# Attention and feed-forward on one core: local units by pairs, turned with 32-row transfers and VectorE from the fourth batch on

## The chip, the cores and the metric

The kernel runs on one core of one Trainium2 chip. The time is device time in microseconds (us), from the start of the program to its end. The core has five engines that run side by side, each with its own queue in program order: TensorE (PE in the profile; PEld are its weight loads), VectorE (DVE), ScalarE (ACT), GpSimd (POOL) and SyncE (SP), which issues all transfers here. TensorE writes into PSUM only.

## The reference, cut to what matters

There are 8 batches of 8 heads, 576 positions and 64 numbers a head. Each batch gets two attentions, whose outputs are added: one over means of 4 neighbouring positions, repeated 4 times, and a local one, in which a position sees those less than 4 away. The sum goes through a feed-forward layer with a gate of its own.

```python
q_d, k_d, v_d = means over 4 positions
out_up = np.repeat(sm_attn(q_d, k_d, v_d), 4, axis=2)
mask = np.abs(pos[:, None] - pos[None, :]) < 4
scores = np.where(mask, scale * (q @ k.T), -1e9)
out_local = softmax(scores) @ v
x = (out_up + out_local)                 # 4608 tokens, 512 wide
h = x @ w_in                             # 1024 wide
solu = h * softmax(h)
ln = (solu - mean) / np.sqrt(var + 1e-6) * g_ln
return ln @ w_out
```

## The kernel before

**Feed-forward.** The 4608 tokens are 36 tiles of 128. `ffn_in(i)` makes h_i with 24 matmuls of 128x512 (L770): x and w_in are each split into a high part and a rest, and three of the four products are kept (xh·wi_h, xh·wi_l, xl·wi_h). VectorE takes the maximum of a row (nmx, L778), ScalarE the exponential (e, L782), VectorE the product with h (L785); then the PSUM tile h, of which there is one, is free for the next tile. The mean is taken off (L807), and the tile goes to memory and back in another order (u, L813, and v, L845), where VectorE turns it in blocks of 32x32 (L866). `ffn_ut` splits it (uh on ScalarE, L872; the rest ul, L874, on GpSimd, on VectorE from tile 29 on), and `ffn_out(i)` makes o_i with 24 matmuls (L888). ScalarE scales the result (osb, L895).

**Local attention.** A window is 64 positions; a unit is two windows, and a batch has five units. `Local.by_tensor` works on one unit, all 8 heads: 16 matmuls of 64x64 for the scores (sc, L614), the mask added by VectorE (L632), the maximum (L637), its subtraction on GpSimd (L639), the exponential (L641), the sum and its reciprocal (L644, L648), the product on GpSimd (L650). Then TensorE turns the probabilities with four transposes of 128x128 (plt, L660), ScalarE copies them out of PSUM (plT, L663), 16 matmuls of 64 rows by 58 or 56 columns multiply them with v (xp, L670), and the result goes into x (L496 or L498). `Local.by_blocks` stands in the source, but `ON_TENSOR = 8` sends every batch to `by_tensor`.

**Pooled attention** goes by pairs of heads (`Pooled`: sd L696, mxd L703, pd L711 and L720, pdt L731, pdT L738 to L743, po L752). The sums of four v are made by GpSimd (`pooled_vsum`, L434 and L437). Batches 0 and 1 get q and k turned by TensorE (qp, kp, L478), the others by VectorE (L411, L415).

**Weights.** `Weights.piece` turns 16 pieces of the float64 weights into a high part and a rest, with four steps on VectorE (L325 to L338), a product with g_ln for w_out (L358), a rounding (L360) and a difference on GpSimd (L362).

**Order.** The program is a list of small steps (`plan`), and the table `ORDER` says by number in which order they are issued. Every engine runs its own instructions in that order and waits where an input isn't there. Two matmuls of zeros at 24 places (`keep_clock`, L947) keep TensorE at work early on.

Of the kernel before, what the change touches and what calls it, by code (L numbers as in the profile page):

```python
# [129 lines left out]
def pooled_local_attention_then_solu_ffn(  # L130
# [34 lines left out]
    QN = SD // QC  # L165


    TILES = ((0, 0), (1, 1), (0, 1), (1, 0))

    EARLY = 2  # L170
    MASKED = 0
    W_PSUM = False
    WARM = 24

    def rows(n):
        return slice(n * 64, n * 64 + 64)

# [864 lines left out]
```

## Time and profile before

| | |
|---|---|
| median of 3 runs | 602.74 us (602.57 to 603.37) |
| profiled execution | 602.74 us, of which the span from the first to the last instruction is 601.0 us |
| ACT busy | 361.8 us, 60% of the span |
| POOL busy | 375.6 us, 62% |
| transfers | 203,913 packets, 94.34 MB, 157 GB/s on average |
| granted TensorE clock | 0.989 on average |

Busy time is time in which an engine has an instruction at work. Busy alone does not say that an engine sets the time: that is read from whether it waits, and from who waits for it.

### The profile page before, as it was taken

Reading aid. Unit: us, or ns where it says so; the run is one execution under the profiler, and the core shown is the slowest. Engines: PE = TensorE matmul, PEld = TensorE weight load, DVE = VectorE, ACT = ScalarE, POOL = GpSimd, SP = SyncE. Lnnn points to the kernel's source line nnn. Section 1 sums busy time; section 2 is a strip of 40 time slices with the busy share of each in tenths; the row PEclk is TensorE's granted clock in tenths of the full one; section 3 lists DMA queues with packets and bytes.
Section 4 is the critical chain, followed back from the end, with each engine's and each line's share of the span. In section 5 each row is a group of like instructions: output and inputs, shape, how many; then the busy total and the mean of one; then the engine's idle time right before and its main releaser. Section 6 shows DMA issues by size and latency. Waiting matters only on the chain.

```text
span 601.0 us, 15341 instructions
## 1 busy us (share of the span) xinstructions
PE 574.8 (96%) x5912; PEld 447.1 (74%) x5912; DVE 396.5 (66%) x692; ACT 361.8 (60%) x800; POOL 375.6 (62%) x553
## 2 busy tenths in 40 slices
PE   6889789899999999999999999999999999999996
PEld 3666557677777777787877777777777878788785
DVE  5989999869747677766856767737655533643541
ACT  3758866577745566566664854657465655553443
POOL 2576668867784778678574777656786767332221
PEclk8979999899999999999999999999999999999999
DMA  8999776687769767766878567847416623124230
GB/s 231 238 251 254 140 183 146 164 178 162 195 144 189 171 167 186 170 148 175 190 151 201 143 173 182 185 114 195 97 59 188 146 89 114 63 88 151 96 123 35
DMA packets 203913, 94.34 MB, mean 157 GB/s; under 512 B 162496, under 2 KB 192704, under 8 KB 203840
## 3 DMA queue, kind: packets, MB, share of 16 engines
q1 hardware_dynamic: 203840, 93.37, 63.3%
q8 instruction: 46, 0.75, 0.6%
q14 instruction: 27, 0.22, 0.1%
HBM read 65.54 MB, written 27.79 MB: 155 GB/s over the span
## 4 chain that ended last, share of the span: by engine, by line
PE 75%; POOL 6%; DVE 5%; ACT 4%; SPq 4%; DMA 3%; issue 3%; POOLq 0%; DVEq 0%
PE o L888 31%; PE h L770 27%; PE xp L670 3%; PE plt L660 3%; PE po L752 3%; PE sc L614 2%; DMA qm<-in_q_dram 2%; SPq L245 2%; PE pdt L731 2%; PE sd L696 2%; POOL pl L639 2%; DMA v<-u 1%; SPq L264 1%; POOL pd L720 1%; DVE w L334 1%
## 5 line engine op out<-in xcount | busy, mean ns | idle before, releaser
L888 PE MATMUL o<-wo_h,uh 128*128 128x512 f32 x288 | 117.9, 409 | 0.8 <-ACT uh L872 0.7
L770 PE MATMUL h<-wi_h,xh 128*128 128x512 f32 x288 | 116.3, 404 | 0.6 <-DVE e L785 0.6
L770 PE MATMUL h<-wi_h,xl 128*128 128x512 f32 x288 | 114.3, 397 | 1.3 <-POOL xl L922 1.3
L888 PE MATMUL o<-wo_l,uh 128*128 128x512 f32 x288 | 114.5, 398 | 0.0
L770 PE MATMUL h<-wi_l,xh 128*128 128x512 f32 x288 | 114.1, 396 | 0.0
L874 POOL TENSOR_TENSOR ul<-v,uh 128x512 fp32r<-128x512 f32 x58 | 74.4, 1288 | 19.7 <-ACT uh L872 7.7
L778 DVE TENSOR_REDUCE nmx<-h 128x1 f32<-128x1024 f32 x36 | 43.9, 1219 | 63.8 <-PE h L770 63.8
L888 PE MATMUL o<-wo_h,ul 128*128 128x512 f32 x288 | 79.1, 396 | 0.4 <-DVE ul L874 0.4
L782 ACT ACTIVATE e<-h,nmx 128x1024 f32<-128x1024 f32 x36 | 40.0, 1112 | 51.0 <-DVE nmx L778 51.0
L888 PEld LDWEIGHTS o<-wo_h,uh 128*128 128x128 f32 x288 | 54.6, 190 | 15.6 <-ACT uh L872 1.4
L770 PEld LDWEIGHTS h<-wi_h,xl 128*128 128x128 f32 x288 | 54.2, 188 | 15.2 <-POOL xl L922 2.1
L770 PEld LDWEIGHTS h<-wi_h,xh 128*128 128x128 f32 x288 | 54.2, 188 | 14.8 <-issue 1.0
L888 PEld LDWEIGHTS o<-wo_h,ul 128*128 128x128 f32 x288 | 54.2, 188 | 14.0 <-DVE ul L874 0.8
L770 PEld LDWEIGHTS h<-wi_l,xh 128*128 128x128 f32 x288 | 54.3, 189 | 12.2
L888 PEld LDWEIGHTS o<-wo_l,uh 128*128 128x128 f32 x288 | 54.5, 189 | 11.8
L922 POOL TENSOR_TENSOR xl<-x,xh 128x512 fp32r<-128x512 f32 (+1 forms) x40 | 47.1, 1183 | 18.6 <-ACT xh L919 17.4
L807 ACT ACTIVATE e<-e,nmu 128x1024 f32<-128x1024 f32 x35 | 40.1, 1146 | 28.2 <-POOL nmu L790 28.1
L785 DVE SCALAR_TENSOR_TENSOR e<-h,e 128x1024 f32<-128x1024 f32 x36 | 43.7, 1214 | 19.9 <-ACT e L782 19.9
L650 POOL TENSOR_TENSOR pl<-pl,rsl 128x512 f32<-128x512 f32 x40 | 42.1, 1055 | 20.7 <-DVE rsl L648 18.2
L866 DVE STREAM_TRANSPOSE v<-v 128x512 f32<-128x512 f32 x70 | 46.3, 688 | 12.5 <-DMA v<-u 12.5
L872 ACT ACTIVATE uh<-v 128x512 fp32r<-128x512 f32 x70 | 42.9, 623 | 14.9 <-DVE v L866 11.0
L639 POOL TENSOR_TENSOR pl<-pl,mxl 128x512 f32<-128x512 f32 x40 | 41.8, 1052 | 9.0 <-DVE mxl L637 4.6
(95 smaller groups left out, 1076.1 us busy)
## 6 DMA issues: line engine op xcount, KB each, us to landing
u<-e SPq DMA_DIRECT2D x35, 512.0 KB
v<-u SPq DMA_DIRECT2D x140, 128.0 KB
vw<-in_v_dram SPq DMA_DIRECT2D x160, 64.0 KB
vs<-in_v_dram SPq DMA_DIRECT2D x32, 288.0 KB
out_dram<-osb SPq DMA_DIRECT2D x36, 256.0 KB
qm<-in_q_dram SPq DMA_DIRECT2D x96, 72.0 KB
km<-in_k_dram SPq DMA_DIRECT2D x96, 72.0 KB
w<-in_moe_w_out_dram SPq DMA_DIRECT2D x8, 512.0 KB
```

What stands on the lines that cost most here:

```text
L639: nc.gpsimd.tensor_tensor(out=pl, in0=pl, in1=max_bc, op=ALU.subtract)
L650: nc.gpsimd.tensor_tensor(out=pl, in0=pl, in1=rs.unsqueeze(3).broadcast_to([P, NPR, 2, W]), op=ALU.mult)
L770: nc.tensor.matmul(hps[:, n, :], src[:, cc, :], wt[:, cc, n * 512:(n + 1) * 512], start=(cc == 0 and src is xh and wt is wi_h), stop=(cc = ...
L778: nc.vector.tensor_reduce(out=nmx, in_=hf, op=ALU.max, axis=AX.X, negate=True)
L782: nc.scalar.activation(e, hf, AF.Exp, bias=nmx, scale=1.0, accum_out=se)
L785: nc.vector.scalar_tensor_tensor(out=e, in0=hf, scalar=1.0, in1=e, op0=ALU.mult, op1=ALU.mult, accum_out=su)
L807: nc.scalar.activation(e, e, AF.Identity, bias=nmu, scale=1.0)
L866: nc.vector.transpose(vg, vg)
L872: nc.scalar.activation(uh, tp, AF.Copy)
L874: (nc.vector if v is None or i in LATE else nc.gpsimd).tensor_tensor(out=ul, in0=tp, in1=uh.bitcast(F32), op=ALU.subtract)
L888: nc.tensor.matmul(o, src[:, j, :], wt[:, 4 * g + j, :], start=(g == 0 and j == 0 and src is uh and wt is wo_h), stop=(g == 1 and j == 3 a ...
L922: nc.gpsimd.tensor_tensor(out=l, in0=src, in1=h.bitcast(F32), op=ALU.subtract)
```

## The change

- For batches 3 to 7 units 0 and 1, and 2 and 3, go through a new class, `PairOfLocals`, two units at a time; unit 4 stays with `Local`. The scores of both units go into one tile `pl` of 128x1024, ordered by halves of 32 keys. Eight transfers of 32 rows by 512 numbers (64 KB each) bring each 32-row block to its place in `plT`, and one VectorE instruction of 128x1024 turns it in blocks of 32x32. The TensorE transposes of those units and the copies out of PSUM are gone; the product with v is 64 columns wide instead of 58. `by_blocks` is removed.
- `MASKED = 2`: in batches 0 and 1 TensorE adds the mask to the scores with two matmuls of 128x256; VectorE takes the maximum from PSUM and subtracts it, and GpSimd's subtraction falls away.
- `G_LATE`: for w_out the product with g_ln and the rounding are one ScalarE instruction, and the rest is one VectorE instruction.
- `OTHER` lists 133 steps in which an instruction goes to the other engine of two. With it GpSimd gives VectorE 27 of 58 `ul`, 19 of 40 `xl`, 11 of 32 `pd`, 10 of 32 pooled sums, and 14 subtractions and products of the local attention; ScalarE gives VectorE 14 of 39 first copies into x, 7 of 35 `e` less the mean, 2 `plT` and 2 `kT`, and takes 6 `pdT`; VectorE gives GpSimd 10 of the first steps (L325) of the 16 pieces of weights.
- `ORDER` is a new table from its first number to its last. The matmuls that keep TensorE at work now use the identity, and each place has a PSUM tile of its own name.

```diff
 ORDER = """
-181 0 182 1 2 3 165 25 183 166 4 5 6 184 167 185 24 26 186 187 188 27 7 8 173 32 168 169 170
+8 0 23 168 169 22 170 171 172 173 174 25 24 10 175 160 161 162 163 164 176 177 16 26 27 32 28
...
+OTHER = """
+37 53 59 93 178 186 202 210 242 250 258 266 274 282 471 482 524 541 543 549 566 568 574 643 671
...
-    MASKED = 0
+    MASKED = 2
...
+    def engine(usual, instead):
+        return instead if now[0] in other else usual
...
-                nc.scalar.activation(t, t, AF.Copy, scale=self.g[:, fc:fc + 1])
+                if G_LATE:
+                    nc.scalar.activation(hi, t, AF.Copy, scale=g)
+                    yield
+                    nc.vector.scalar_tensor_tensor(
+                        out=lo, in0=t, scalar=g, in1=hi.bitcast(F32), op0=ALU.mult, op1=ALU.subtract
+                    )
...
-    ON_TENSOR = 8
+    PAIRED = 3
...
+    class PairOfLocals:
...
+            pl = big(f"pl_{b}_{u}")
+            by_unit = pl.rearrange("p (c n h k) -> p c n h k", c=2, n=2, k=32)
+            for n in range(2):
...
+                        nc.tensor.matmul(
+                            at[rows(wi), par, pr],
+                            bt.qT[rows(par), pr, s0:s0 + W], bt.kT[rows(par), pr, s0:s0 + W],
+                            start=True, stop=True,
+                        )
...
+            plT = big(f"plT_{b}_{u}")
+            half = N * 32
+            for wi in range(2):
+                for a in range(2):
+                    for c in range(2):
+                        nc.sync.dma_start(
+                            plT[wi * 64 + c * 32:][0:32, a * half:(a + 1) * half],
+                            pl[wi * 64 + a * 32:][0:32, c * half:(c + 1) * half],
+                        )
+                yield
+            nc.vector.transpose(plT, plT)
+            yield
...
+                        nc.tensor.matmul(
+                            xp[rows(par), wi, pr * W:(pr + 1) * W],
+                            bt.vw[u + n][rows(wi), 2 * pr + par, :],
+                            plT[rows(wi), n, par * NPR + pr], start=True, stop=True,
+                        )
...
-            (nc.vector if v is None or i in LATE else nc.gpsimd).tensor_tensor(
+            usual = nc.vector if v is None or i in LATE else nc.gpsimd
+            (usual if v is None else engine(usual, nc.vector)).tensor_tensor(
                 out=ul, in0=tp, in1=uh.bitcast(F32), op=ALU.subtract
```

Three places show how the order moves. The last number of a name is that of its buffer; the two before it are the batch and the unit (or head pair), or the tile and its half.

**TensorE, between the output matmuls of tile 12 and the next input matmuls.** Before, the end of batch 4's local attention and the start of batch 5's:

```order
L670 MATMUL xp_4_2_4383<-plT_4_2_4259,vw_4_2_4041 64x58 x16
L660 MATMUL plt_4_3_4403<-ident_82,pl_3_108 128x128 x4
L670 MATMUL xp_4_1_4410<-plT_4_1_4127,vw_4_1_3485 64x58 x16
L614 MATMUL sc_5_1_4429<-kT_5_4137,qT_5_4321 64x64 x16
L660 MATMUL plt_4_4_4464<-ident_82,pl_0_105 128x128 x4
L670 MATMUL xp_4_3_4475<-plT_4_3_4408,vw_4_3_3570 64x58 x16
L614 MATMUL sc_5_0_4499<-kT_5_4137,qT_5_4321 64x64 x16
```

Now, at the same place, in the middle of tile 12's output:

```order
L753 MATMUL xp_4_2_4274<-plT_4_2_4120,vw_4_2_3310 64x64 x16
L607 MATMUL sc_5_4_4306<-kT_5_3930,qT_5_4117 64x64 x16
L655 MATMUL plt_4_4_4325<-ident_82,pl_0_107 128x128 x4
L823 MATMUL pdt_4_0_4331<-ident_82,pd_4_0_4100 72x64 x12
L695 MATMUL sc_5_0_4354<-kT_5_3930,qT_5_4117 64x2x32 x16
```

Of the transposes `plt` only that of unit 4 is left; the product `xp` of unit 2 is 64 columns wide.

**VectorE, from the maximum of tile 18 to the product that frees h.** Before:

```order
L778 TENSOR_REDUCE nmx_18_5044<-h_18_4939 128x1
L411 STREAM_TRANSPOSE kT_6_5055<-km_6_4452 128x576
L367 TENSOR_REDUCE kd_6_5057<-kT_6_5055 128x144
L411 STREAM_TRANSPOSE kT_6_5055<-km_6_4452 128x576 x2
L785 SCALAR_TENSOR_TENSOR e_18_5066,su_18_5069<-h_18_4939,e_18_5066 128x1024
```

Now, with the three instructions ahead of the maximum:

```order
L746 STREAM_TRANSPOSE plT_5_0_4865<-plT_5_0_4865 128x1024
L972 TENSOR_TENSOR ul_15_0_4877<-v_15_4781,uh_15_0_4876 128x512
L719 TENSOR_TENSOR pl_5_2_4757<-pl_5_2_4757,mxl_5_2_4818 128x1024
L870 TENSOR_REDUCE nmx_18_4927<-h_18_4893 128x1
L963 STREAM_TRANSPOSE v_16_4879<-v_16_4879 128x4x128
L913 RECIPROCAL r_16_4942<-se_16_4544 128x1
L639 TENSOR_REDUCE sml_5_4_4961<-pl_1_108 128x8
L643 RECIPROCAL rsl_5_4_4963<-sml_5_4_4961 128x8
L1020 TENSOR_TENSOR xl_19_4940<-x_4_4231,xh_19_4939 128x512
L972 TENSOR_TENSOR ul_15_1_4889<-v_15_4781,uh_15_1_4888 128x512
L913 RECIPROCAL r_17_4982<-se_17_4812 128x1
L877 SCALAR_TENSOR_TENSOR e_18_4994,su_18_4997<-h_18_4893,e_18_4994 128x1024
```

Three instructions that stood on GpSimd (`ul` twice and `xl`) are now in VectorE's row, two of them between maximum and product; ahead of the maximum stand a turn of `plT`, which waits for transfers, and a subtraction of 128x1024.

**SyncE at the same place**, where the transfers of `plT` stand. Now:

```order
L942 DMA v_15_4781<-u_15_4536 32x4x256 x4
L299 DMA vw_7_2_4846<-in_v_dram 64x8x64 x2
L741 DMA plT_5_0_4865<-pl_5_0_4353 32x512 x8
L942 DMA v_16_4879<-u_16_4775 32x4x256 x4
L286 DMA qm_6_4495<-in_q_dram 32x18x32 x4
L286 DMA km_6_4496<-in_k_dram 32x18x32 x4
```

Before, the transfers of v_16 followed loads of v and the output of tile 12:

```order
L264 DMA vw_6_4_4848<-in_v_dram 64x4x64 x4
L897 DMA out_0_dram<-osb_12_4518 128x512
L264 DMA vw_5_3_4864<-in_v_dram 64x4x64 x4
L845 DMA v_16_4933<-u_16_4844 32x4x256 x4
L264 DMA vw_5_1_4957<-in_v_dram 64x4x64 x4
```

The eight transfers stand ahead of those of v_16 and wait for the product of the pair on its engine; a load of `vw` now takes two transfers instead of four.

More of the change, by code (lines that the diff above doesn't have):

```diff
@@ L208, in pooled_local_attention_then_solu_ffn, with make_bands @@
         nc.vector.tensor_copy(out=mask_b, in_=mask)
-    if WARM:
-        zeros = cpool.tile([P, P], BF16, name="zeros")
-        nc.gpsimd.memset(zeros, 0.0)
+    if MASKED:
+        filler = ident_b
+    elif WARM:
+        filler = cpool.tile([P, P], BF16, name="filler")
+        nc.gpsimd.memset(filler, 0.0)
     mhalf = cpool.tile([P, 1], F32, name="mhalf")
     nc.vector.memset(mhalf, -0.5)
+    GR = SD // 2
+    BAND = {0: (0, 16), 1: (3, 15), 3: (1, 15)}
+    bands = {}
+    def make_bands():
+        t = moe.tile([P, DFF], F32, tag="e", name="bands")[:, 0:3 * 160]
+        t = t.rearrange("p (r x) -> p r x", r=3)
+        nc.gpsimd.memset(t, 0.0)
+        by_half = ident.rearrange("p (h k) -> p h k", h=2)
+        for n, (r, (off, m)) in enumerate(BAND.items()):
+            nc.vector.tensor_reduce(
+                out=t[:, n, GR:GR + m],
+                in_=by_half[:, :, off:off + FAC * m].rearrange("p h (j i) -> p j h i", i=FAC),
+                op=ALU.add, axis=AX.XY,
+            )
+            bands[r] = t[:, n]
     LP = 2 * W + 2
@@ L223, in pooled_local_attention_then_solu_ffn, with copy @@
     nc.vector.memset(qd_flat[:, NPR * SD:], 0.0)
+    other = {int(n) for n in OTHER.split()}
+    now = [None]
+    def engine(usual, instead):
+        return instead if now[0] in other else usual
+    def copy(eng, out, in_):
+        if eng is nc.scalar:
+            nc.scalar.activation(out, in_, AF.Copy)
+        else:
+            eng.tensor_copy(out=out, in_=in_)
     def two_banks(pool, tag, name):
@@ L433, in pooled_vsum, with pool_steps @@
             vs = self.vs.pop((c, hs.start))
[L434 removed]
+            eng = engine(nc.gpsimd, nc.vector)
+            eng.tensor_tensor(
                 out=vs[:, :, 0:2 * D], in0=vs[:, :, 0:2 * D], in1=vs[:, :, 2 * D:4 * D], op=ALU.add
             )
[L437 removed]
+            eng.tensor_tensor(
                 out=self.vd[:, c, hs], in0=vs[:, :, 0:D], in1=vs[:, :, D:2 * D], op=ALU.add
             )
+        def pool_steps(self):
+            firsts = [-(-s0 // FAC) for s0 in starts]
+            ends = firsts[1:] + [SD]
+            for c in range(2):
+                tp = two_banks(ps_h, "h", f"vp_{self.b}_{c}")[0:GR]
+                at = tp.rearrange("p h (r a d) -> p h r a d", r=NPR, a=2)
+                ws = range(5 * c, 5 * c + 5)
+                for w in ws:
+                    s0, g0, g1 = starts[w], firsts[w], ends[w]
+                    at0 = GR - (g0 - GR * c)
+                    K = FAC * g1 - s0
+                    for half in range(2):
+                        nc.tensor.matmul(
+                            at[:, half, :, half ^ (w % 2), :],
+                            bands[s0 % FAC][half * W:half * W + K, at0:at0 + GR],
+                            self.vw[w // 2][half * W:half * W + K, w % 2],
+                            start=w == ws[0], stop=w == ws[-1],
+                        )
+                yield
+                vd = self.vd[:, c].rearrange("p h d -> p (h d)")
+                nc.scalar.activation(vd, tp[:, 0], AF.Copy)
+                yield
+                nc.vector.tensor_tensor(out=vd, in0=vd, in1=tp[:, 1], op=ALU.add)
+                yield
     class EarlyBatch(Batch):
@@ L806, in ffn_in @@
         else:
-            nc.scalar.activation(e, e, AF.Identity, bias=nmu, scale=1.0)
+            if engine(nc.scalar, nc.vector) is nc.scalar:
+                nc.scalar.activation(e, e, AF.Identity, bias=nmu, scale=1.0)
+            else:
+                nc.vector.tensor_scalar(
+                    out=e, in0=e, scalar1=1.0, scalar2=nmu, op0=ALU.mult, op1=ALU.add
+                )
         s = small.tile([P, 1], F32, tag="s", name=f"s_{i}", bufs=6)
@@ L940, in pooled_local_attention_then_solu_ffn @@
     weights = Weights()
-    idle = []
     def keep_clock(n):
-        if not idle:
-            idle.append(ps_o.tile([P, 512], F32, tag="o", name="warm"))
+        o = ps_o.tile([P, 512], F32, tag="o", name=f"warm_{n}")
         for _ in range(2):
             nc.tensor.matmul(
-                idle[0].rearrange("p (a n) -> p a n", n=P), zeros,
-                zeros.unsqueeze(1).broadcast_to([P, 4, P]), start=True, stop=True,
+                o.rearrange("p (a n) -> p a n", n=P), filler,
+                filler.unsqueeze(1).broadcast_to([P, 4, P]), start=True, stop=True,
             )
@@ L981, in attention @@
     def attention(bt):
-        values(bt)
-        local = [Local(bt, u, bt.b > 0) for u in range(5)]
-        pooled = [Pooled(bt, pr, bt.b == 0) for pr in range(NPR)]
-        for it in pooled + local if bt.b == 0 else local + pooled:
-            if isinstance(it, Local):
+        by_pe = bt.b < SUMS_ON_PE
+        late = bt.b == 0
+        if bt.b < PAIRED:
+            local = [Local(bt, u, not late) for u in range(5)]
+        else:
+            local = [PairOfLocals(bt, 0, not late), PairOfLocals(bt, 2, not late), Local(bt, 4, not late)]
+        pooled = [Pooled(bt, pr, late) for pr in range(NPR)]
+        if by_pe:
+            if not bt.b:
+                step(make_bands)
+            for u in range(5):
+                step(bt.load_v, u)
+            row(bt.pool_steps(), 6)
+        else:
+            values(bt)
+        for it in pooled + local if late else local + pooled:
+            if isinstance(it, PairOfLocals):
+                step(bt.load_v, it.u)
+                step(bt.load_v, it.u + 1)
+                row(it.steps(), 16)
+                continue
+            if isinstance(it, Local) and not by_pe:
                 step(bt.load_v, it.u)
```

206 lines of the change are left out of this document (103 added, 103 removed), and 199 rows, old and new, of tables (ORDER, OTHER).

## The prediction

> **What bounds the kernel now.** I read the page's busy shares first, then the busy times of chosen stretches, then the chain of work that ended last. In the stretches each engine has its busy time and, in brackets, its instructions; after them stand TensorE's granted clock and the share of the transfer engines.
>
> ```profile
> span 601.0 us, 15341 instructions
> PE 574.8 (96%) x5912; PEld 447.1 (74%) x5912; DVE 396.5 (66%) x692; ACT 361.8 (60%) x800; POOL 375.6 (62%) x553
> ...
> 0.00:120.00 120.00, 100.16 (x1546) 74.08 (x1547) 106.38 (x182) 79.46 (x182) 77.54 (x89) 0.94 0.85 201
> 120.00:555.00 435.00, 433.63 (x4192) 340.84 (x4191) 272.28 (x484) 262.88 (x587) 290.07 (x439) 1.00 0.62 152
> ...
> 20.00:60.00 40.00, 34.78 (x687) 26.79 (x684) 36.10 (x67) 30.15 (x89) 25.75 (x25) 0.91 1.02 247
> 60.00:110.00 50.00, 41.18 (x558) 31.21 (x550) 48.94 (x82) 36.65 (x75) 35.91 (x38) 1.00 0.73 162
> ...
> 142.40:354.30 211.90, 211.56 (x2156) 166.46 (x2154) 142.57 (x253) 131.88 (x299) 148.89 (x218) 1.00 0.73 172
> ```
>
> From 120 to 555 us TensorE is idle for 435 - 433.6 = 1.4 us: it is the bound there, and what leaves its queue leaves the time. A busy share alone wouldn't say so, since matmuls overlap, but the chain agrees, with TensorE at 75% of the span. The first 120 us are another stage: TensorE is idle for 20 us, transfers are at their limit up to 60 us (share 1.02), and VectorE is at 98% from 60 to 110 us (48.94 of 50).
>
> ```profile
> PE 75%; POOL 6%; DVE 5%; ACT 4%; SPq 4%; DMA 3%; issue 3%; POOLq 0%; DVEq 0%
> ```
>
> I sum against the execution's own time of 602.74 us: a span of 601.0 and 1.7 around it. It is also the median of the three runs.
>
> **Transposes that go.** Start times of TensorE groups (start, length, line):
>
> ```profile
> 360.45 0.66 PE L660 MATMUL plt<-ident,pl 128*128 128x128 f32 x4
> 361.04 1.16 PE L614 MATMUL sc<-kT,qT 64*64 64x64 f32 x64
> 362.13 0.66 PE L660 MATMUL plt<-ident,pl 128*128 128x128 f32 x4
> 362.71 0.69 PE L670 MATMUL xp<-plT,vw 64*64 64x56 f32 x32
> 363.33 0.50 PE L888 MATMUL o<-wo_h,uh 128*128 128x512 f32 x1
> ...
> 350.81 0.66 PE L660 MATMUL plt<-ident,pl 128*128 128x128 f32 x4
> 351.22 0.47 PE L888 MATMUL o<-wo_h,uh 128*128 128x512 f32 x1
> ```
>
> From start to next start, the four transposes of a unit take 0.41 to 0.59 us. Five batches lose them for four units each: 20 x 0.5 = **-10.0 us** (-8.2 to -11.8). All of them fall after 120 us, in the stage that TensorE bounds. The product xp takes 0.62 us at 56 columns (362.71 to 363.33); the scores, with 64, take 1.09 / 2 = 0.55. Width hardly shows; going by 64/58 of 0.5, I add 20 x 0.04 = **+0.8** (0 to 1.4). That the new scores are written in runs of 32 I cost at nothing, as no row shows such a write.
>
> **Early masks.** Each of ten units gets two matmuls of 128x256 in bf16. The nearest row:
>
> ```profile
> 20.73 1.90 PE L947 MATMUL warm<-zeros 128*128 128x512 bf16 x8
> 22.56 1.21 PE L478 MATMUL qp<-ident,qm 96*64 96x96 f32 x24
> ```
>
> (22.56 - 20.73) / 8 = 0.23 us for 512 columns, so 0.115 for 256, and 20 of them take 2.3 us. They lie where TensorE has 20 us to spare; about half will hide: **+1.2** (0 to 2.3).
>
> **The start.** What leaves the path there is GpSimd's subtraction in batches 0 and 1. Pieces of the chain:
>
> ```profile
> 2.10 8.49 DMA qm<-in_q_dram
> ...
> 31.93 1.00 POOL pl L639
> ...
> 33.80 0.97 POOL pl L639
> ...
> 35.90 2.00 POOL pl L639 x2
> ...
> 111.24 3.81 PE o L888 x12
> ```
>
> Four of them, 4.0 us, stand in the chain. The first q also gets one 512 KB piece of weights less ahead of it on SP; it now lands 8.5 us after the start, with 1.6 MB up to and including it, so a third less is worth up to 2.7 us. Against it, VectorE, 98% busy, receives eight rests of w_out (8 x 0.77 = 6.1 us) and gives ten first steps (10 x 0.81 = 8.1 us), but gets copies and differences too: counted up to the second half of o_0 its order holds some 4 us more than before. Between -6 (both gains in full) and +4 (VectorE's extra in full) I take **-2.5**, nearer the gains because four of these links are in the chain by name.
>
> **VectorE.** This is the unknown term. Its rows:
>
> ```profile
> L866 DVE STREAM_TRANSPOSE v<-v 128x512 f32<-128x512 f32 x70 | 46.3, 688 | 12.5 <-DMA v<-u 12.5
> L632 DVE TENSOR_TENSOR pl<-sc,mask 128x512 f32<-128x512 f32 x40 | 26.7, 675 | 12.8 <-PE sc L614 12.7
> L498 DVE TENSOR_TENSOR x<-x,xp 128x464 f32<-128x464 f32 x4 | 2.5, 624 | 0.4 <-PE xp L670 0.4
> L325 DVE TENSOR_SCALAR w<-w 128x512 f32<-128x512 f32 x16 | 12.9, 814 | 5.6 <-ACT w L323 5.6
> L874 DVE TENSOR_TENSOR ul<-v,uh 128x512 fp32r<-128x512 f32 x12 | 9.0, 765 | 7.6 <-ACT uh L872 5.5 <-issue 2.1
> ```
>
> Over the whole program it gains: 10 turns of 128x1024 at 2 x 0.688 (13.8 us); 27 ul and 19 xl, six of them halves, 43 x 0.765 (32.9); 14 subtractions and products, seven of double width, 21 x 0.675 (14.2); 11 pd of 432 columns (6.3); ten pairs of pooled sums, 1.5 x 0.675 each (10.1); 14 copies into x and 4 others (11.4); 7 e of double width (9.5); w_out 6.1. It loses 8.1 of L325 and six copies pdT (2.7). Sum: +93 us on 396.5. Neighbours overlap a little (two turns in a row take 1.31 us, not 1.38), so some +88.
>
> ```profile
> 133.34 1.31 DVE v L866 x2
> ```
>
> It is not spread evenly. From the start of h_5 (142.4 us) to that of h_20 (354.3) VectorE was busy for 142.6 of 211.9 us. In the new order the same stretch of tiles holds 15 ul, 4 xl, 5 wide turns, 14 halves of subtraction or product, 6 pd, 5 pooled sums, 6 copies, 2 e and some ten turns and sums of q, k and v that come earlier: by the rows above 54, with the overlap 51 us. TensorE's stretch loses ten transposes and shrinks to about 207 us. So VectorE stands at 194 of 207, 94%, where it was at 67%. GpSimd falls from 149 to about 101 and ScalarE loses 22 copies; they can't be the bound.
>
> What that costs depends on how full VectorE can run. The stretch from 60 to 110 us shows 98%: 194 / 0.98 = 198, under 207, and costs nothing. That from 20 to 60 us shows 36.10 of 40, 90%: 194 / 0.9 = 215, and costs 8. I take the middle, **+4** (0 to 22, see the third rival).
>
> Where it would bite: h has one PSUM tile, so h_19 waits for VectorE's product on h_18.
>
> ```profile
> L778 DVE TENSOR_REDUCE nmx<-h 128x1 f32<-128x1024 f32 x36 | 43.9, 1219 | 63.8 <-PE h L770 63.8
> L785 DVE SCALAR_TENSOR_TENSOR e<-h,e 128x1024 f32<-128x1024 f32 x36 | 43.7, 1214 | 19.9 <-ACT e L782 19.9
> ...
> 222.88 5.62 PE o L888 x24
> ```
>
> Between h_18 and h_19 TensorE has only o_15, 5.62 us. VectorE's maximum and product take 2.4; between them the order has a turn (0.69), a sum (0.68), xl and ul (1.53) and three reciprocals (0.5): 5.8 us, some 5.5 with the overlap. So there the slack is gone, where the old order had sd, pdt and plt as well. Tiles 9, 13, 20 and 23 have as little. The turn of plT also waits on VectorE for its transfers, with ul_15 and the maximum behind it. The nearest transfers, the four of v with the same 512 KB, took 5.45 us in the chain; waits for v cost VectorE 12.5 us in all (the row of L866).
>
> ```profile
> 318.20 5.45 DMA v<-u
> ```
>
> On SP the eight transfers wait for the pair's product, with v_16, q and k queued behind; before tile 20 such a delay meets tiles of slack, so I put it inside the +4.
>
> **Sum.** 601.0 - 10.0 + 0.8 + 1.2 - 2.5 + 4 = 594.5; with the 1.7 around it **596 us**.
>
> **Rivals.** *First, nothing waits.* The transposes are worth their upper end (-11.8), VectorE keeps up (0) and the start gains 4: 601 - 11.8 + 0.8 + 1.2 - 4 = 587.2, so 589 us (584 to 591). For it: TensorE ran 435 us with 1.4 idle while VectorE waited for h alone for 63.8 us, so there is slack to spend. Against it: the 94%.
>
> *Second, the saving comes back as waiting.* TensorE loses its 10 us of work and waits 8 to 13 us longer; time 600.5 to 604.5. This is also the case where transposes are swapped for waits on transfers and the change does not do what it says.
>
> *Third, slower: VectorE and GpSimd shut each other out.* Four rows of the timeline:
>
> ```profile
> 537.18 1.29 POOL L922 TENSOR_TENSOR xl<-x,xh 128x512 fp32r<-128x512 f32 x1
> 537.99 1.63 DVE L874 TENSOR_TENSOR ul<-v,uh 128x512 fp32r<-128x512 f32 x2 [0.23 <-ACT uh L872]
> ...
> 558.37 1.30 POOL L922 TENSOR_TENSOR xl<-x,xh 128x512 fp32r<-128x512 f32 x1 [3.48 <-ACT xh L919]
> 558.96 1.27 DVE L874 TENSOR_TENSOR ul<-v,uh 128x512 fp32r<-128x512 f32 x1
> ```
>
> The VectorE ul at 558.96 takes 1.27 us; it ends at 560.23, 0.56 after GpSimd's xl ends at 559.67. At 537.99 the first of two lasts until about 0.6 after GpSimd's end as well. A difference of two SBUF tiles on VectorE seems to start only when GpSimd is through, which costs 0.5 to 0.6 us. From h_5 to h_20 the new order has some 43 such instructions, where the old had none, while GpSimd is busy half the time: 43 x 0.5 x 0.56 = 12 us. VectorE then needs 206 of 207 us, and at the 90% of 20 to 60 us 229: +22 instead of +4, which gives 614; at 94% it is +12 and 604. It decides from about 12 us of extra waiting; I put its price at 608 us.
>
> The Trainium skill says the same more broadly, in "SBUF — State Buffer", section "Who interferes with whom": a VectorE instruction with two SBUF inputs contends with a GpSimd instruction that reads SBUF, and the second to issue blocks until the first is finished. The two cases above agree. By that rule moved work costs GpSimd waits too, and the sum leans to the third rival; by VectorE's mean row (0.765, hardly any waiting) it stays at 596.
>
> **How the numbers follow.** Forecast (591 to 600.5) 0.50; first rival 0.18; second 0.12, half of it within 0.2% and nearly all the rest faster; third 0.20. The range 586 to 608 leaves out about 0.05 below and 0.12 above, with the end set by the unknown waits on VectorE. A measurement of this kernel can tell some 0.2% from no change, that is 601.5 to 603.9: faster 0.73, same 0.06, slower 0.21.
>
> **What would show it.** Right: 80 transposes L660 left, TensorE's work after 120 us some 9 us less and its idle time there 3 to 8 us instead of 1.4, ended mostly by VectorE (e on h, xl, ul); VectorE near 485 us busy, over 90% from tile 5 to 20. The start: the second half of o_0, which began at 111.2 us (the last piece shown of the start), no later than that. Wrong: TensorE still without idle time (first rival); ul and xl on VectorE at 0.9 us or more on average and TensorE idle for over 12 us (third); or TensorE slower in the new scores or products, which nothing here prices.

## The result, and the profile after

The changed kernel takes 599.93 us (median of 5 runs, 599.04 to 600.81) against 603.13 us (5 runs, 602.57 to 604.32): ratio 0.9944, 95% interval 0.9927 to 0.9961. Measured again beside 22 runs of the kernel before (e5 below) the ratio is 0.9962 (0.9943 to 0.9980). It is faster by 2 to 3 us, a third to a half of the 6.7 forecast. Four single runs in a slower state (two of the kernel before, one each of e6 and e8) are left out of the medians in this text. Its profiled execution took 600.81 us, 599.0 of it the span.

The page of the changed kernel: span, busy time, share and instructions of each engine, then the shares of the chain that ended last.

```profile
span 599.0 us, 15199 instructions
PE 567.2 (95%) x5852; PEld 434.6 (73%) x5852; DVE 487.0 (81%) x792; ACT 330.7 (55%) x743; POOL 285.2 (48%) x433
...
PE 64%; DVE 13%; DMA 7%; issue 4%; POOL 4%; SPq 4%; ACT 3%; DVEq 0%; POOLq 0%; ACTq 0%
```

TensorE has 7.6 us less busy time, VectorE 90 us more: 487 where the prediction wrote 485. In the chain TensorE falls from 75% to 64% and VectorE rises from 5% to 13%. The busy times by stretch, in the stretches that the prediction used (the last one is h_5 to h_20 again):

```profile
0.00:120.00 120.00, 97.67 (x1521) 69.01 (x1522) 112.03 (x185) 70.20 (x166) 77.69 (x77) 0.99 0.80 197
120.00:555.00 435.00, 431.10 (x4166) 335.32 (x4165) 358.85 (x582) 242.03 (x547) 200.19 (x332) 1.00 0.66 166
20.00:60.00 40.00, 32.45 (x658) 23.17 (x657) 38.86 (x69) 29.74 (x88) 29.20 (x23) 1.00 0.93 228
60.00:110.00 50.00, 42.55 (x529) 30.71 (x531) 48.16 (x77) 28.35 (x61) 35.41 (x35) 1.00 0.65 145
141.40:357.40 216.00, 213.24 (x2191) 166.63 (x2188) 191.73 (x312) 125.27 (x287) 105.54 (x172) 1.00 0.78 184
```

From 120 to 555 us TensorE is idle for 3.9 us (435 - 431.1) where it was 1.4. VectorE was at 191.7 us from h_5 to h_20, against 194 forecast. That stretch took 216.0 us, not 207, since the new order puts more of TensorE's instructions into it (2191, where it was 2156); so VectorE's share is 89% there, not the 94% forecast. From 20 to 60 us it is now 97% busy (38.86 of 40), where it was 90%.

**Where the 2 us of the span come from** is seen best by cutting both traces at the start of h_4. Up to there they issue the same TensorE work, except that the new one has the 20 mask matmuls and one `sd` less. h_4 starts at 128.3 us before and at 131.4 after. Before:

```profile
0.00:128.30 128.30, 108.46 (x1665) 80.33 (x1666) 113.11 (x194) 84.74 (x194) 82.14 (x95) 0.95 0.85 199
...
128.30:601.00 472.70, 466.31 (x4249) 366.80 (x4248) 283.40 (x499) 277.10 (x606) 293.42 (x459) 1.00 0.58 146
```

After:

```profile
0.00:131.40 131.40, 109.07 (x1673) 77.26 (x1674) 120.96 (x202) 78.14 (x182) 84.07 (x88) 0.99 0.79 193
...
131.40:599.00 467.60, 458.17 (x4181) 357.37 (x4179) 366.06 (x591) 252.58 (x562) 201.15 (x346) 1.00 0.62 159
```

From h_4 on the change gains 472.7 - 467.6 = 5.1 us: TensorE has 8.1 us less work and is idle 3.0 us longer. That is the forecast (10.0 - 0.8 less, 4 longer: 5.2). Up to h_4 it loses 3.1 us, where the forecast had -2.5 for the start and +1.2 for the masks, a gain of 1.3. In these two traces the whole miss of 4.4 us lies there. VectorE has 7.85 us more busy time up to h_4 (120.96 - 113.11). The prediction counted some 4 up to the second half of o_0; up to there it is 8.5 (99.40 us of the 111.2 before, 107.86 of the 115.8 after).

The 3.1 us are the difference of two traces, and not a measured price of the new order: h_4 doesn't start at one time in all traces of one order. With the old order up to h_4 it starts at 127.2 to 132.9 us (before, e1, e10, e16, e18), with the new one at 130.7 to 132.1 (the changed kernel, e2, e5, e11).

**Why so much more than 4.** The steps of the weights on VectorE, before and after (count, busy time, mean in ns). Before, beside L325 with its 12.9 us, which the prediction shows:

```profile
L329 DVE TENSOR_SCALAR w<-w 128x512 int32<-128x512 int32 x16 | 9.2, 587 | 0.2
L338 DVE SCALAR_TENSOR_TENSOR w<-w,w 128x512 int32<-128x512 int32 x12 | 8.0, 683 | 0.1
L334 DVE SCALAR_TENSOR_TENSOR w<-w,w 128x512 int32<-128x512 int32 x12 | 8.0, 682 | 0.1
L334 DVE SCALAR_TENSOR_TENSOR w<-stage,w 128x512 int32<-128x512 int32 x4 | 3.7, 928 | 0.1
L338 DVE SCALAR_TENSOR_TENSOR w<-stage,w 128x512 int32<-128x512 int32 x4 | 3.7, 926 | 0.1
```

After, where L366 is the first step, L370, L375 and L379 the other three:

```profile
L366 POOL TENSOR_SCALAR w<-w 128x512 f32<-128x512 f32 x10 | 19.9, 1994 | 9.9 <-DMA km<-in_k_dram 3.9 <-ACT w L364 3.7 <-ACT mxd L799 2.1
L370 DVE TENSOR_SCALAR w<-w 128x512 int32<-128x512 int32 x16 | 13.1, 821 | 2.5 <-POOL w L366 2.3
L375 DVE SCALAR_TENSOR_TENSOR w<-w,w 128x512 int32<-128x512 int32 x12 | 10.4, 865 | 0.1
L379 DVE SCALAR_TENSOR_TENSOR w<-w,w 128x512 int32<-128x512 int32 x12 | 9.5, 798 | 0.0
L366 DVE TENSOR_SCALAR w<-w 128x512 f32<-128x512 f32 x6 | 4.5, 758 | 3.2 <-ACT w L364 3.2
L375 DVE SCALAR_TENSOR_TENSOR w<-stage,w 128x512 int32<-128x512 int32 x4 | 3.3, 827 | 0.1
L379 DVE SCALAR_TENSOR_TENSOR w<-stage,w 128x512 int32<-128x512 int32 x4 | 2.8, 689 | 0.1
```

The sums are 45.5 us before and 43.6 after. Ten of the 16 first steps left VectorE, 8.1 us at its own mean, and it has only 1.9 us less, since the steps that stayed became longer: L329, 0.587 us, is now 0.821. The timeline shows how. VectorE of the changed kernel (start, length):

```profile
60.96 1.49 DVE L370 TENSOR_SCALAR w<-w 128x512 int32<-128x512 int32 x1
62.37 1.12 DVE L366 TENSOR_SCALAR w<-w 128x512 f32<-128x512 f32 x1
63.42 1.53 DVE L375 SCALAR_TENSOR_TENSOR w<-w,w 128x512 int32<-128x512 int32 x1
...
66.07 0.41 DVE L370 TENSOR_SCALAR w<-w 128x512 int32<-128x512 int32 x1
```

GpSimd beside it:

```profile
60.90 1.27 POOL L1020 TENSOR_TENSOR xl<-x,xh 128x512 fp32r<-128x512 f32 x1
62.13 1.09 POOL L812 TENSOR_TENSOR pd<-pd,rsd 128x432 f32<-128x432 f32 x1
63.18 1.22 POOL L645 TENSOR_TENSOR pl<-pl,rsl 128x512 f32<-128x512 f32 x1
```

Three steps in a row on VectorE end 0.28, 0.27 and 0.55 us after the GpSimd instruction that runs beside them, at 1.1 to 1.5 us each; L370 at 66.07, with GpSimd idle, takes 0.41. The waiting stands inside the busy time, so the groups show no idle time for it. The Trainium skill, "SBUF — State Buffer", section "Who interferes with whom", has the rule: besides instructions with two SBUF inputs, `tensor_scalar` can take the ports that VectorE shares with GpSimd, and who issues first keeps them to the end of its instruction. These rows agree.

### The profile page after: what moved, and what is told of

Read it like the earlier page. It is cut to its first block, busy times and chain, and to the rows that moved or that the text cites. A ratio compares the mean times of both kernels' runs of the same rounds, so it can differ in the third digit from the quotient of the medians.

```text
span 599.0 us, 15199 instructions
## 1 busy us (share of the span) xinstructions
PE 567.2 (95%) x5852; PEld 434.6 (73%) x5852; DVE 487.0 (81%) x792; ACT 330.7 (55%) x743; POOL 285.2 (48%) x433
## 4 chain that ended last, share of the span: by engine, by line
PE 64%; DVE 13%; DMA 7%; issue 4%; POOL 4%; SPq 4%; ACT 3%; DVEq 0%; POOLq 0%; ACTq 0%
PE o L986 27%; PE h L862 25%; PE po L844 2%; PE sd L788 2%; DMA w<-in_moe_w_in_dram 2%; DMA vw<-in_v_dram 2%; DMA qm<-in_q_dram 1%; PE pdt L823 1%; SPq L286 1%; PE xp L753 1%; SPq L305 1%; PE sc L695 1%; PE xp L665 1%; DVE nmx L870 1%; POOL w L366 1%
## 5 line engine op out<-in xcount | busy, mean ns | idle before, releaser
L862 PEld LDWEIGHTS h<-wi_h,xl 128*128 128x128 f32 x288 | 54.1, 188 | 14.7 <-POOL xl L1020 1.5
L972 POOL TENSOR_TENSOR ul<-v,uh 128x512 fp32r<-128x512 f32 x31 | 40.1, 1299 | 46.4 <-ACT uh L969 37.1
L993 ACT ACTIVATE osb<-o,s 128x512 f32<-128x512 f32 x36 | 24.5, 680 | 35.6 <-PE o L986 22.2
L882 POOL TENSOR_SCALAR nmu<-su 128x1 f32<-128x1 f32 x36 | 9.3, 257 | 70.3 <-DVE e L877 63.5
L900 ACT ACTIVATE e<-e,nmu 128x1024 f32<-128x1024 f32 x28 | 32.1, 1146 | 16.8 <-POOL nmu L882 16.8
L919 ACT ACTIVATE e<-e 128x1024 f32<-128x1024 f32 x35 | 36.7, 1049 | 2.2 <-DMA u<-e 2.2
```

The lines of the kernel that those rows point to most:

```text
L862: nc.tensor.matmul(hps[:, n, :], src[:, cc, :], wt[:, cc, n * 512:(n + 1) * 512], start=(cc == 0 and src is xh and wt is wi_h), stop=(cc = ...
L900: nc.scalar.activation(e, e, AF.Identity, bias=nmu, scale=1.0)
L919: nc.scalar.activation(e0, e, AF.Square, accum_out=m2)
L972: (usual if v is None else engine(usual, nc.vector)).tensor_tensor(out=ul, in0=tp, in1=uh.bitcast(F32), op=ALU.subtract)
L993: nc.scalar.activation(osb, o, AF.Copy, scale=s)
```

## The experiments

All carry times beside runs of the kernel before on the same chip; its medians were 602.4 to 603.9 us. "Changed" is 600.3 us (e5) where a difference is formed.

**e1 and e2: halves exchanged.** At h_4 the two tables have done nearly the same steps, so they can be joined there. e1 sets `MASKED = 0` and `G_LATE = False`, takes the order of before up to h_4 and the new order for all that is left; e2 sets `PAIRED = 8` and does the opposite.

> All steps ahead of the first half of h_4 go in the order and on the engines of before (mask added by VectorE, w_out with the product apart, no step on its other engine); from there on everything as changed. Theory 1, the start is where the forecast gain was lost (some 3 us more there in the changed trace, against a forecast of 1.3 less): 596 us, 594 to 598, with o_0's second half near 111 us again. Theory 2, the loss lies behind the start, in the waits for VectorE: 599 to 601, as the changed kernel.

> The other way round: all steps ahead of the first half of h_4 as changed, from there on the order and the engines of before, with no pairs at all. Theory 1: slower than before by 3 to 5 us, 606 to 608. Theory 2: the start is no loss, 601 to 603.5.

e1: 601.50 us, ratio 0.9975 (0.9950 to 1.0000). e2: 608.09 us, 1.0106 (1.0075 to 1.0137). e2 is as theory 1 expects: with the new start alone the kernel is slower. Of the 5.4 us of its trace's span 3.3 lie up to h_4 and 2.1 behind it.

e1 missed both numbers and doesn't confirm theory 1. Its trace has the old order up to h_4 and still reaches h_4 only at 131.7 us, as late as the changed kernel, with a granted clock of 0.91 up to there; e10, also with the old order up to h_4, reaches it at 127.4:

```profile
0.00:131.70 131.70, 113.94 (x1664) 83.57 (x1665) 113.18 (x194) 84.79 (x194) 81.76 (x95) 0.91 0.82 193
...
0.00:127.40 127.40, 105.84 (x1665) 79.26 (x1665) 113.19 (x195) 84.94 (x194) 82.02 (x94) 0.96 0.87 200
```

VectorE's load is the same in both. From h_4 on e1's trace takes 469.2 us, 1.6 more than the changed kernel, all of it idle time of TensorE. Its 12 runs go from 597.25 to 603.75 with the mean granted clock: the five at 0.99 or above average 598.9, the other seven 602.4. At 0.99 or above the changed kernel averages 600.3 (14 runs) and the kernel before 601.8 (17 runs). So the old start is ahead only where the clock is high; these are groups picked afterwards.

**e3 and e4: steps back on their old engines, order kept.**

```diff
 OTHER = """
-37 53 59 93 178 186 202 210 242 250 258 266 274 282 471 482 524 541 543 549 566 568 574 643 671
+178 186 202 210 242 250 258 266 274 282 541 543 566 568 574 643 671 675 692 695 697 699 711 723
...
```

```diff
 OTHER = """
...
+37 53 59 93 178 186 202 210 242 250 258 266 274 282 471 482 524 549 683 716
```

> The changed kernel, with only the steps ahead of h_5 that were given to VectorE (two kT copies, six copies into x, one pooled sum, xl_4 and xl_5, one subtraction and one product) back on ScalarE and GpSimd; GpSimd keeps its ten first steps of the weights. Theory 1 in the form that these instructions fill VectorE, which is 97% busy there: 2 to 4 us under the changed kernel, 596 to 598. If it is the order of the start or the early masks on TensorE instead: within 1 us of the changed kernel, 599 to 601. Theory 2: the same.

> The changed kernel, with all steps behind h_5 back on the engines they had before (ul, xl, pd, pooled sums, products on GpSimd, copies and e on ScalarE); pairs, turns and order stay. VectorE loses some 65 us of work behind the start. Theory 2 (waits for a full VectorE and for the two engines that shut each other out cost about 4 us there): 594 to 597. Theory 1: VectorE was not the bound there; GpSimd and ScalarE take it back at no more than 2 us either way, 598 to 602. A third: these moves are what lets the chains of a unit keep up, and without them TensorE waits: 603 or more.

e3: 608.42 us, 1.0106 (1.0079 to 1.0133); e4: 617.66 us, 1.0256 (1.0225 to 1.0286). Both contradict theory 1 as it was put: less work on VectorE, and slower; e4 is the third case of its expectation. The waits show why. In e3, between 20 and 75 us (who waited, for whom, us, times, longest):

```profile
PE sd L787 <- ACT kT L262: 3.5, 1, 3.5
PE qp L556 <- ACT kT L262: 2.2, 1, 2.2
```

A copy of kT on ScalarE stands there behind a rounding of w_out, which waits for VectorE. In e4, behind h_4:

```profile
PE h L855 <- POOL xl L1013: 8.3, 6, 5.0
```

The old engines no longer fit the new order. An undone move with the order kept tests the fit as much as the load, so e13, e14, e15 and e17 take work out and give it to nobody.

**e5: the changed kernel again.**

> The changed kernel as it is, measured again beside the next runs and with as many runs of before, since the runs of before and of the start of before spread over 6 to 7 us and follow the granted clock. If the gain is of the orders: ratio 0.993 to 0.9965. If the first measurement owed it to a luckier clock: nearer to 1, with the clock of the changed kernel no higher than that of before.

600.34 us (12 runs, 599.39 to 602.93), ratio 0.9962 (0.9943 to 0.9980): the gain stands. Its mean clock, 0.992, is above that of the runs of before beside it, 0.982.

**e6, e7, e14, e17: the ten first steps.** They were given back to VectorE (e6), moved alone in the kernel before (e7), and taken out of both (e14, e17). e7 and, where `n` is one of the ten, e17:

```diff
-            nc.vector.tensor_scalar(
+            (nc.gpsimd if n in (2, 3, 5, 6, 10, 11, 12, 13, 14, 15) else nc.vector).tensor_scalar(
                 out=t, in0=t, scalar1=F64_LO, scalar2=F64_HI, op0=ALU.max, op1=ALU.min
             )
```

```diff
+            if n not in (2, 3, 5, 6, 10, 11, 12, 13, 14, 15):
+                nc.vector.tensor_scalar(
                     out=t, in0=t, scalar1=F64_LO, scalar2=F64_HI, op0=ALU.max, op1=ALU.min
                 )
```

> The changed kernel, with the ten first steps of the weights that went to GpSimd back on VectorE. Theory A (in the start GpSimd and VectorE hold each other up: in the changed trace the other three steps of the weights on VectorE take 7 us more than before, less 1.3 on the staged pieces, so the move freed only some 2 of the 8.1 us that were forecast): VectorE's work up to h_4 rises by 2 to 3 us only, its other steps fall back to about 0.6 to 0.7 us each, and the time stays within 2 us of the changed kernel (598 to 602). Theory B (the move freed its 8.1 us, the loss has another cause): VectorE's work rises by 8 us in a start that it bounds, 604 to 608.

> The kernel before, with one edit: the same ten first steps on GpSimd. Theory A: VectorE's other three steps of the weights grow to 0.75 to 0.85 us each, its work up to h_4 falls by 3 us at most, and GpSimd, with 20 us more, delays its own chains: no gain, 602 to 606. Theory B: 8.1 us less on VectorE, half of it on the path: 597 to 600.

> The changed kernel without the ten first steps of the weights on GpSimd (the bounds on the magnitude, which these pieces then lack). GpSimd loses 19 us up to h_4 and VectorE nothing of its own. If GpSimd holds VectorE up through them: VectorE's other steps of the weights fall from 0.80 to 0.87 us to under 0.75, its sum up to h_4 by 3 to 5.6 us, and the time by 2 to 5 us, 595 to 598. If the lengthened steps come from other GpSimd work: both stay, 599 to 600.5.

> The kernel before without the ten first steps of the weights (the bounds on the magnitude, which these pieces then lack). VectorE has 8.1 us less up to h_4 and nobody more. If VectorE's load reaches the time at the 0.75 of e13 (5.9 us out, 4.4 us won): 6 us under before, 595.5 to 598. If the old start was not bound by VectorE as the new one is: 600 to 602.5. Either way far from e7, where the same ten steps on GpSimd made it 16 us slower.

| the ten steps stand on | order of before | order of the change |
|---|---|---|
| VectorE | 602.4 to 603.9 us | e6: 601.48 us, 0.9963 (0.9937 to 0.9989) |
| GpSimd | e7: 619.10 us, 1.0265 (1.0238 to 1.0291) | e5: 600.34 us, 0.9962 (0.9943 to 0.9980) |
| nobody | e17: 598.67 us, 0.9927 (0.9901 to 0.9954) | e14: 596.69 us, 0.9901 (0.9864 to 0.9938) |

Taken out, the ten steps are worth 4.5 us in the old order (beside the 603.19 of its own runs of before) and 3.7 to 4.8 in the new. Moved to GpSimd they are worth nothing in the new order (e6 and e5 can't be told apart) and cost 16 us in the old one. Of e7:

```profile
L325 POOL TENSOR_SCALAR w<-w 128x512 f32<-128x512 f32 x10 | 19.3, 1936 | 5.9 <-ACT w L323 5.8
L329 DVE TENSOR_SCALAR w<-w 128x512 int32<-128x512 int32 x16 | 15.7, 994 | 14.8 <-POOL w L325 14.7
```

The step behind the moved one waits 14.7 us for GpSimd and is lengthened from 0.587 to 0.994 us besides; the six rows of the weights' steps on VectorE sum to 48.3 us, more than the 45.5 with all 16 first steps. Theory A holds on the time in e6 and e7. In e6, which keeps the order of the change, the six rows sum to 44.9 us, where the changed kernel has 43.6: within one order the move freed 1.3 us. But the steps behind the first one didn't fall back to 0.6 to 0.7 us as theory A had it:

```profile
L368 DVE TENSOR_SCALAR w<-w 128x512 int32<-128x512 int32 x16 | 10.3, 646 | 0.3
L364 DVE TENSOR_SCALAR w<-w 128x512 f32<-128x512 f32 x16 | 9.9, 621 | 3.3 <-ACT w L362 3.3
L377 DVE SCALAR_TENSOR_TENSOR w<-w,w 128x512 int32<-128x512 int32 x12 | 9.4, 787 | 0.0
L373 DVE SCALAR_TENSOR_TENSOR w<-w,w 128x512 int32<-128x512 int32 x12 | 9.2, 770 | 0.1
```

In e14, too, only half of its expectation holds: the time fell by 3.7 us, but of the three steps only the first came down.

```profile
L379 DVE SCALAR_TENSOR_TENSOR w<-w,w 128x512 int32<-128x512 int32 x12 | 11.4, 954 | 0.0
L375 DVE SCALAR_TENSOR_TENSOR w<-w,w 128x512 int32<-128x512 int32 x12 | 10.4, 870 | 0.1
L370 DVE TENSOR_SCALAR w<-w 128x512 int32<-128x512 int32 x16 | 9.2, 574 | 0.1
```

So the 3.9 us on L370 come from the moved steps; the lengthening of L375 and L379 stayed, so other work beside them lengthens them; the row at 63.42 us above, L375 beside GpSimd's L645, is one such case. Up to h_4 VectorE's busy time falls by only 1.9 us (121.06 in e5, 119.13 here; 3 to 5.6 were expected), GpSimd's by 20.2:

```profile
0.00:130.90 130.90, 113.16 (x1673) 80.47 (x1674) 119.13 (x202) 77.95 (x182) 63.75 (x78) 0.95 0.79 193
```

h_4 isn't earlier in this trace; its execution, 600.07 us, is the second slowest of six. How much of e14's gain is GpSimd's own queue and how much is VectorE isn't separated.

**e8, e12, e13: w_out.** e8 sets `G_LATE = False`. e12 does so too, has the ten first steps on VectorE and the end of e11. e13 leaves the rests out:

```diff
-                    nc.vector.scalar_tensor_tensor(
-                        out=lo, in0=t, scalar=g, in1=hi.bitcast(F32), op0=ALU.mult, op1=ALU.subtract
-                    )
...
-            for src, wts in ((uh, (wo_h, wo_l)), (ul, (wo_h,))):
+            for src, wts in ((uh, (wo_h, wo_h)), (ul, (wo_h,))):
```

> The changed kernel, with product, rounding and rest of w_out as before: one more ScalarE instruction a piece (8 x 0.63 us), the eight rests on GpSimd (8 x 1.3 us) and off VectorE (8 x 0.74 = 5.9 us). If what VectorE was given fills the start (theory 1): 2 to 4 us faster than the changed kernel, 596 to 598. Theory A: GpSimd's 10 us more come back as longer VectorE steps and waits of the weights: 600 to 604.

> The changed kernel with the tail of e11, the ten first steps back on VectorE and w_out as before (product apart, rests on GpSimd). Without the ten steps GpSimd has 19 us less up to h_4, so the rests (10.4 us) no longer wait behind them as in e8, and VectorE has 5.9 us less than in e6. Theory 1 (what VectorE is given fills the start): 594 to 598. Theory A: the rests on GpSimd hold VectorE up, and ScalarE's eight products (5 us) stand in the chain of each piece: 600 to 606.

> The changed kernel without the eight rests of w_out on VectorE (5.9 us up to h_4); the output matmuls read the high part in their place, as many as before, so the output lacks the rest's share. No other engine gets the work. If VectorE's load sets the start (97% busy): h_4 comes 3 to 6 us earlier, 594 to 597.5. If chains through several engines set it and VectorE only looks full: less than 1.5 us, 599 to 600.5.

e8: 612.54 us, 1.0155 (1.0121 to 1.0189). e12: 608.13 us, 1.0099 (1.0069 to 1.0129). e13: 596.02 us, 0.9889 (0.9860 to 0.9918). e8 and e12 are slower than any of their expectations. In e8, up to h_4, GpSimd waits at the rests for ScalarE, whose second instruction of a piece now stands in between, and what is queued behind a rest waits with it:

```profile
POOL wo_l L411 <- ACT wo_h L409: 19.0, 5, 5.9
```

e13 is the clearer test: 5.9 us of VectorE's work taken out and given to nobody win 4.3 us. Busy time up to h_4 in e5 and then in e13 (VectorE is the third number):

```profile
0.00:130.70 130.70, 109.49 (x1672) 77.16 (x1673) 121.06 (x202) 78.15 (x182) 83.99 (x88) 0.99 0.79 193
```

```profile
0.00:130.90 130.90, 113.27 (x1672) 80.08 (x1673) 117.40 (x194) 77.70 (x182) 81.76 (x88) 0.95 0.80 193
```

VectorE's busy time falls by 3.7 us. h_4 isn't earlier in this trace: it is of the slowest of e13's six executions (600.21 us; the other five took 594.9 to 596.1), with TensorE's clock at 0.95 up to h_4. The times carry the verdict here, the trace only the load. In e17 a fall of 4.5 us (113.11 to 108.59) goes with 4.5 us of time, and h_4 comes 2.3 us earlier in its trace:

```profile
0.00:126.00 126.00, 108.37 (x1665) 81.06 (x1666) 108.59 (x184) 84.59 (x194) 81.69 (x95) 0.93 0.86 203
```

**e9 and e15: the masks.** e9 sets `MASKED = 0` with the new order, each addition right ahead of its maximum; unit 4 of batch 0 is then written over unit 0 before that is used. e15 drops the loop `if early:` with its two matmuls.

> The changed kernel, with the masks of batches 0 and 1 added by VectorE again: 20 matmuls less on TensorE, the ten subtractions back on GpSimd; the matmuls that keep TensorE at work still use the identity. Theory A (GpSimd and VectorE hold each other up in the start): GpSimd's 10.6 us more lengthen VectorE's steps of the weights and each unit's chain, 603 to 610. The rival, that the masks on TensorE (0.16 us each from start to start, 3.2 us) are what the start lost: 596 to 598.

> The changed kernel without the 20 matmuls that add the mask in batches 0 and 1; their scores stay unmasked, so the output of these batches is another. TensorE loses 3.2 us from start to start, in a start where it waits 21 us. If TensorE's work sets the start: 3 us less, 596.5 to 598. If half hides, as the forecast took: 1 to 2 us less. If VectorE sets it: 0 to 0.7, 599.5 to 600.5.

e9: 622.36 us, 1.0332 (1.0303 to 1.0362). It can't be read: 9.1 of its 20 us are one wait of TensorE for an addition that the order doesn't fit. e15: 602.62 us, 0.9994 (0.9973 to 1.0016). Taking the mask matmuls out gains nothing; they are not what the start lost. That it is 2 us slower than the changed kernel goes with a lower clock (mean 0.985 over its runs) and isn't explained further.

**e10: the identity alone.**

```diff
-        nc.gpsimd.memset(zeros, 0.0)
+        nc.vector.tensor_copy(out=zeros, in_=ident)
```

> The kernel before, with one edit: the matmuls that keep TensorE at work multiply the identity instead of zeros, as in the change. If the data decide the granted clock of the first 40 us (1.00 in all six traces with the identity up to 30 us, 0.5 to 0.66 somewhere between 10 and 20 us in both with zeros): no dip there, and 1 to 3 us faster than before, 600 to 602. If the dip follows TensorE's wait of 2.8 us for the first q, which the identity doesn't shorten: dip and time stay, 602 to 605.

601.86 us, 0.9997 (0.9977 to 1.0018). No dip of the clock up to 30 us, though TensorE waits for the first q as before; mean clock 0.990 against 0.986 beside it. The time is the same. So the higher clock of the changed kernel isn't shown to be part of its gain.

**e11, e16, e18: what could be added.** e11 puts the steps from h_34 on into the old order. e16 is e1 with the identity and that end; e18 is e16 joined at h_5.

> The changed kernel, with the steps behind the first half of h_34 in the order of before (h_35 in two halves around o_33): its o_34 and o_35 waited 0.3 and 1.3 us for ScalarE's scaling of the output before them, the old order 0.7 once. Expected: from h_34 to the end 0.7 to 1.1 us less, 599 to 600 beside 600.3 of the changed kernel; nothing if the waits only move.

> As e1 (start of before, later part of the change), with the identity for the matmuls that keep TensorE at work and the tail of e11. e1's runs followed the granted clock: 598.9 on average at 0.99 or more, 602.3 below. If the identity keeps the clock up: mean clock 0.99 or more and 597 to 599, faster than both kernels. If the clock dips as often as before: 599.5 to 601.

> As e16, but with the order and engines of before up to the first half of h_5 instead of h_4. Behind the join TensorE waited 6.8 us in e1 against 5.5 in the changed kernel. If that is of the join: 597 to 599, under both kernels again. If the later part needs what the changed start has done ahead by then: 600 to 603.

e11: 599.86 us, 0.9951 (0.9935 to 0.9968); from the start of h_34 to that of o_35 its trace takes 29.8 us, that of e5 30.9. The 1.1 us are there, too little to show in the time. e16: 598.73 us, 0.9921 (0.9896 to 0.9946), the best that computes everything; it beats the kernel before, but its interval overlaps that of the changed kernel, so the lead of 1.6 us on that one is not shown. e18: 601.39 us, 0.9972 (0.9947 to 0.9996). Its trace reaches h_4 at 127.2 us, but takes 472.4 from there on, 4.8 more than that of e5; 4.2 of them are one wait of TensorE for a copy into x on ScalarE. That fits the second case of its expectation.

## Why the prediction was half right

- **Transposes, -10.0.** Right. 80 are left, and from h_5 on the groups of TensorE, from start to next start, give 14.0 us for the 29 old ones and 5.2, half a microsecond of it waiting, for the 10 left: some 9 less.

```profile
L655 PE MATMUL plt<-ident,pl 128*128 128x128 f32 x80 | 12.9, 284 | 2.3 <-ACT plT L263 1.1 <-POOL pl L645 1.0 <-DVE plT L265 0.2
L746 DVE STREAM_TRANSPOSE plT<-plT 128x1024 f32<-128x1024 f32 x10 | 12.3, 1227 | 0.2
```

The ten turns wait 0.2 us in all: the eight transfers of each are there in time, against the second rival.

- **VectorE behind the start, +4.** Right in size: TensorE is idle 3.0 us longer from h_4 on.
- **Third rival, the mutual exclusion from h_5 on.** Wrong there: its mark was 0.9 us on average.

```profile
L972 DVE TENSOR_TENSOR ul<-v,uh 128x512 fp32r<-128x512 f32 x39 | 29.3, 751 | 8.2 <-ACT uh L969 7.6 <-POOL s L926 0.2
L1020 DVE TENSOR_TENSOR xl<-x,xh 128x512 fp32r<-128x512 f32 x13 | 8.8, 675 | 2.2 <-ACT xh L1017 2.2
```

Rows of the start show it (those at 60.96 to 63.42 us above), where the prediction didn't look for it.

- **Early masks, +1.2.** A cost isn't shown: without the matmuls nothing is gained (e15).
- **The start, -2.5: the step that failed.** The prediction says that VectorE "gives ten first steps (10 x 0.81 = 8.1 us)" and that "up to the second half of o_0 its order holds some 4 us more than before". A move to GpSimd was counted as if it freed its full length on VectorE and cost nothing on GpSimd. It freed 1.9 us of VectorE's steps (45.5 to 43.6; 1.3 within one order, e6), and it won no time (e6 and e5). GpSimd needs 1.99 us for each step, and VectorE's remaining steps wait for GpSimd in their busy time. The mark that the prediction set, the second half of o_0 no later than 111.2 us, came at 115.8 in the trace.

The size of the error shows in e14. It is the change as the prediction counted it, with the ten steps gone from VectorE at no cost elsewhere, and takes 596.69 us, where 596 were forecast and the changed kernel takes 600.34. By these medians the move alone makes up some 3.7 of the 4.4 us by which the start missed (the two ratios, 0.9864 to 0.9938 and 0.9943 to 0.9980, don't overlap). That e14 meets the forecast so closely is partly luck, since the other terms of the start weren't measured one by one.

The same can be estimated from the load, more roughly. Up to the second half of o_0 it rose by 8.5 us instead of some 4. In e13 and e17 a microsecond of VectorE's busy time was worth about a microsecond of the run (4.3 for 3.7; 4.5 for 4.5). By that rate the extra load costs some 8 us (an estimate), and with h_4 3.1 later the gains in the start are some 5, inside the 6 that the prediction allowed them. One of them is in the trace: the first q product starts at 8.39 us instead of 10.63, 2.2 of the 2.7 hoped for. The 5 itself is a remainder, not measured. And in e14 3.7 us of time went with only 1.9 of VectorE's busy time, so VectorE's load isn't the whole of it.

Of the start's two ends, -6 and +4, the second was mis-sized, then: by this estimate it is near +8. I took a value near the gains because links of GpSimd stood in the chain by name, and the load on a 98% busy engine did not. One rival stays open. The chain that ended last runs through SyncE's issues of transfers from 77.2 to 89.8 us before and from 77.3 to 94.4 after, some 4.5 us longer, and no run changed those transfers alone.

## What to carry to other kernels

On a full VectorE, price a move to GpSimd by what VectorE has left afterwards, not by the length of the moved instruction: look at how the neighbours lengthen while GpSimd is at work, since such waiting is counted as busy. To find which load bounds a stage, take work out and give it to nobody; undoing a move inside an order made for it tests the fit as well (e3, e4, e8 and e12 were all slower), and so can mislead. Cut two traces at a point where both have issued the same work, and compare term by term on each side; but look first how far that point lies apart in traces of one and the same order.

## What was unexpected

- A first step (`tensor_scalar`, maximum and minimum, 128x512, one input) takes 1.99 us on GpSimd, longer than its products with two inputs of the same size (L645, 1.10 us on average). On VectorE the same step takes 0.42 us when GpSimd is idle (L366 at 43.33 us of the changed kernel). The Trainium skill, "GPSIMD Engine Reference", section "4.1 Engine selection", has GpSimd about 2 times slower with two inputs and near line rate with one; here the case with one input is the slower one, and the measurement decides.
- TensorE's granted clock varies from run to run of one kernel within the start, and the time with it: over 94 runs of the kernel before, 2.2 us for each 0.01 of mean clock. Yet e10 raised the mean clock by 0.004 without a gain in time, so the relation isn't shown to be one of cause.
